# GpSimd begins some of the transfers of an attention, FFN and gated-MLP kernel

## The chip, the cores and the metric

The kernel runs on one core of a Trainium2 chip. The metric is the device time of one execution in microseconds (us); lower is better. Three runs of the kernel before gave a median of 1019.06 us (1018.1 to 1020.91). The profile shows five engines: PE (TensorE) with its weight loads (PEld), DVE (VectorE), ACT (ScalarE), POOL (GpSimd) and SP (SyncE), whose only work here is to begin transfers between the chip's large memory and the on-chip buffers. A transfer is carried out by 16 DMA engines that serve whoever began it.

## The reference

Three blocks follow each other, for 4 batches of 448 tokens and 768 features, in float32:

```python
scores = cap * np.tanh(scale * (q @ k.T) / cap)          # 12 heads of 64, per batch
attn = softmax(scores) @ v                               # x = heads side by side
xn = (x - mean) / sqrt(var + 1e-6) * g_ln
x = x + relu(xn @ w_ch1) @ w_ch2                         # 768 -> 3072 -> 768
h = relu(x @ w_in)                                       # 768 -> 1024, halves u and v
v_s = einsum('ts,bsd->btd', w_spatial, norm(v)) + b_spatial
out = (u * v_s) @ w_out                                  # 512 -> 768
```

`w_ch1` and `w_ch2` are called w1 and w2 below. The weights come to the chip as 64-bit values, so each must be turned into float32 there.

## The kernel before

The batches go in two passes, 0 and 1, then 2 and 3. Four stages make up the first half of the run: attention of batches 0 and 1; then the first FFN matrix for those batches together with the attention of batches 2 and 3 (`h_units`, `attend`); then the second FFN matrix of the first pass (`y_seven`); then the gated MLP (`gmlp`). The second pass has no attention of its own left to do.

Precise float32 products are made of three matmuls on a high and a low part of each operand. The two FFN matrices are multiplied by a scheme with seven block products in place of eight. For that `mixed_h` forms, from four blocks of the middle layer (the output of the first FFN matrix), seven mixed blocks in tiles named hx, and stores all seven to the chip's memory as tensors named h. `y_seven` loads them again (`hs<-h`). There are ten hx tiles, and a group of four blocks takes eight of them; a tile is free again only when its store has landed. There are 12 groups, so 84 stores in the first pass.

The rows of w2 are made ready for `y_seven` beside the first FFN matrix (`ahead`, `value`). Each of the 36 rows is loaded raw (512 KB, into one of two tiles w40 and w41), converted by one instruction of ACT (`wc<-w`) and two of DVE into one of two tiles wc, and stored converted (256 KB, `kept_w<-wc`), from where `y_seven` loads it. Raw rows of w1 (768 KB) go the same way with tiles of their own.

What each engine does, and in which order, is fixed when the program is built. `Program.order` gives every instruction a due time, worked back from PE's order with a cost and a latency for each; `Program.plan` plays the program through and lets each engine take the ready instruction that is due first. In the played model all transfers share one stream of 360 GB/s. An engine then runs its list strictly in order: an instruction that waits holds up everything behind it on that engine. SP has one list of 903 entries, and each of its transfers also waits until the eighth transfer before it has landed. All transfers of the kernel before are begun by SP.

Of the kernel before, what the change touches and what calls it, by code (L numbers as in the profile page):

```python
# [12 lines left out]
I32 = mybir.dt.int32  # L13
# [202 lines left out]
class Program:  # L216
# [93 lines left out]
    def order(self):  # L310
        n = len(self.ops)
        pred = self.edges()
        self.pred, self.succ = pred, [[] for _ in range(n)]
        for i, ds in enumerate(pred):
            for j, at in ds.items():
                self.succ[j].append((i, at))
        self.bufs = []
        for i, (_, writes, reads) in enumerate(self.ops):
            mine = list(dict.fromkeys(a.buf for a in chain(writes, reads) if isinstance(a, View)))
            for b in mine:  # L320
                b.first = i if b.first is None else b.first
                b.last = i
                b.uses += 1
            self.bufs.append(mine)
        self.pools = {b.pool for m in self.bufs for b in m}
        total = 0.0
        due = [float("inf")] * n
        for i in range(n):
            engine, cost = self.ops[i][0][0][:2]
            if engine == "PE":  # L330
                due[i] = total
                total += cost
            elif i in self.soon:
                due[i] = total
        for p in self.pools:
            p.reuse()
        for s in self.stages:
            begins = [b for p in s.pools for b in p.bufs if b.first is not None]
            if s.after and begins:
                first = min(begins, key=lambda b: b.first)  # L340
                for a in s.after:
                    for b in (b for p in a.pools for b in p.bufs if not b.after):
                        assert b.last < first.first
                        b.after.append(first)
        for i in reversed(range(n)):
            engine, cost, latency = self.ops[i][0][0][:3]
            latency += 1.4 if engine == "D" else 0.0
            for j, at in chain(self.succ[i], {(a.first, 0.0) for b in self.bufs[i] for a in b.after}):
                due[i] = min(due[i], due[j] + at * SLACK - (cost + latency + self.DELAY) * SLACK)
            if due[i] == float("inf"):  # L350
                due[i] = total
        return self.plan(due)

    def plan(self, due):

        n = len(self.ops)
# [12 lines left out]
        out = []  # L369
# [59 lines left out]
        while True:  # L429
            for e in ready:  # L430
                if busy[e]:
                    continue
                found = pick(e)
                if found is None:
                    continue
                i, k = found
                taken[i] = True
                out.append((i, k))
                for b in bufs[i]:
                    if b.tile is None:  # L440
                        b.pool.take(b)
                busy[e] = True
                cost, latency = self.ops[i][0][k][1:3]
                if e == "PE":
                    spent += cost
                free[e] = now + cost
                if e == "D":
                    moved = max(moved, now + 1.5) + latency
                    latency = moved + 0.77 - now - cost
                heapq.heappush(events, (now + cost, 0, seq, e))  # L450
                done = now + cost + latency + self.DELAY
                for j, at in succ[i]:
                    heapq.heappush(events, (max(now, done - at), 1, seq, j))
                    seq += 1
                heapq.heappush(events, (done, 2, seq, i))
                seq += 1
            if not events:
                rest = [d for q in ready.values() for d, i, _ in q if not taken[i] and d > reach()]
                if not rest:
                    break  # L460
                relief = min(rest)
                continue
            relief = float("-inf")
            now, kind, _, x = heapq.heappop(events)
            if kind == 0:
                busy[x] = False
            elif kind == 1:
                left[x] -= 1
                if not left[x]:
                    release(x)  # L470
            else:
                for b in bufs[x]:
                    b.left -= 1
                    if not b.left:
                        b.pool.give(b)
                        if b.pool.stage is not None and not b.pool.stage.left:
                            for s in b.pool.stage.then:
                                if not s.open and all(not a.left for a in s.after):
                                    s.open = True
                                    out.append((s, None))  # L480
                                    for p in s.pools:
                                        p.changes += 1
# [16 lines left out]
class Recorder:  # L499
# [3 lines left out]
    def __getattr__(self, method):  # L503
# [5 lines left out]
        def record(*args, **kw):  # L509
# [5 lines left out]
            if self.name == "PE":  # L515
                cost = (n / 2400 + 0.0133) * kw["rhs"].ap[0][1] / 128
                if kw["rhs"].dtype == F32:

                    part = kw["rhs"].ap[0][1] * kw["out"].ap[0][1] / 128 ** 2
                    cost = (4 * n / 2400 + 0.004) * part + (0.004 if part < 1 else 0.0)  # L520
            elif self.name == "D":
                cost, latency = 0.5, 4 * out.size() / 360e3
            elif self.name == "A":
                cost = (0.13 if psum_in else 0.16) + n / 1200
                cost += 0.094 if hasattr(kw.get("scale"), "tensor") else 0.0
            elif self.name == "P":
                cost = 1.3 if "pow" in repr(args) + repr(kw) else 0.7 + n / 500
            elif method == "reciprocal":
                cost = 0.15 + n / 160
            elif method in ("tensor_copy", "tensor_scalar") and not psum_in:  # L530
                cost = 0.14 + n / 1920
            else:
                cost = 0.14 + n / 960
# [12 lines left out]
def attn_ffn_gmlp_kernel(  # L546
# [147 lines left out]
    def value(kind, j, home=None, pool=wr):  # L694
# [7 lines left out]
            SP.dma_start(out=t, in_=kept[kind, j])  # L702
        else:
            raw = raw6[0 if n > DH else 2].get()[:, 0:n]
            SP.dma_start(out=raw.rearrange("p n t -> p (n t)"), in_=source[kind][j].bitcast(I32))
            t = pool.get()[:, 0:n]
            ti = t.bitcast(I32)
            hi, lo = raw[:, :, 1], raw[:, :, 0]
# [20 lines left out]
            if kind == "w2":  # L729
                if j % KD == 0:  # L730
                    kept2.append(dram.tile([128, 2, KD, n // 2], F32, name=f"kept_{kind}_{j}"))
                SP.dma_start(out=kept2[j // KD][:, :, j % KD], in_=t.rearrange("p (a n) -> p a n", a=2))
            else:
                d = kept[kind, j] = dram.tile([128, n], F32, name=f"kept_{kind}_{j}")
                SP.dma_start(out=d, in_=t)
# [320 lines left out]
    def mixed_h(i, h11, h12, h21, h22, t1, t2, t3, t4):  # L1056
# [4 lines left out]
        sub(t4, h21, t2)  # L1061
        for n, t in ((1, h11), (3, h22), (2, h21), (5, t1), (6, t2), (7, t3), (4, t4)):
            hidden[n, i] = dram.tile([128, S], F32, name=f"h{int(last_pass[0])}_{n}_{i}")
            SP.dma_start(out=hidden[n, i], in_=t)

    ysp = []

# [743 lines left out]
```

## Time and profile before

| quantity | value |
|---|---|
| median of three runs | 1019.06 us |
| lowest and highest run | 1018.1 and 1020.91 us |
| span of the profiled execution, first to last instruction | 1016.5 us |
| the profiled execution's own time | not recorded; the median lies 2.56 us above its span |
| PE busy | 1002.0 us (99%) |
| DVE busy | 856.2 us (84%) |
| ACT busy | 565.4 us (56%) |
| POOL busy | 24.3 us (2%), 21 instructions |
| moved by the DMA engines | 248.71 MB, mean 245 GB/s |
| TensorE clock granted | full speed throughout (1.000) |

The span is what the profile divides up; the run's time also holds a little before the first and after the last instruction. Busy PE is a union of modelled intervals, so a small wait can hide in it, but an idle stretch of PE that the profile shows is real time lost.

### The profile page before, as it was taken

The page shows a single profiled execution, that of the slowest core. Times are in us where ns is not written, and L with a number is a line of the kernel's source. Part 1 is how long each engine was busy: PE and PEld are TensorE (multiplying, and loading weights), DVE is VectorE, ACT ScalarE, POOL GpSimd, SP SyncE. Part 2 cuts the span into 40 slices and gives each one's busy share as a digit, 9 for nine tenths or more (in the row PEclk, how much of TensorE's full clock was granted, in tenths as well). Part 3 has the DMA queues.
Part 4 walks back from the last instruction along what each step waited for, and adds up shares of the span by engine and source line. Part 5 has one row for each costly group of instructions (what it writes and reads, how often), then busy time and mean ns, then how long its engine had stood idle before and what let it go on. Part 6 is the DMA issues. An engine that isn't in the chain of part 4 may idle for free.

```text
span 1016.5 us, 14927 instructions
## 1 busy us (share of the span) xinstructions
PE 1002.0 (99%) x5056; PEld 825.9 (81%) x5056; DVE 856.2 (84%) x1476; ACT 565.4 (56%) x897; POOL 24.3 (2%) x21
## 2 busy tenths in 40 slices
PE   7999999999999999999999999999999999999998
PEld 2332787787778889999889899999999999998887
DVE  6989998878888779989889989877788777778986
ACT  7999776776667344545566245544465322214553
POOL 0000110000000000000001110000000000000000
PEclk9999999999999999999999999999999999999999
DMA  8454779999999999999684233565799986602402
GB/s 261 154 139 144 256 279 360 359 337 369 338 370 363 358 341 403 409 329 375 244 259 144 50 133 117 165 203 194 236 336 395 337 267 222 192 21 71 132 17 109
DMA packets 132048, 248.71 MB, mean 245 GB/s; under 512 B 21970, under 2 KB 93828, under 8 KB 131972
## 3 DMA queue, kind: packets, MB, share of 16 engines
q1 hardware_dynamic: 131972, 247.76, 70.9%
q8 instruction: 40, 0.66, 0.3%
q14 instruction: 36, 0.29, 0.1%
HBM read 167.70 MB, written 80.01 MB: 244 GB/s over the span
## 4 chain that ended last, share of the span: by engine, by line
PE 75%; DMA 14%; DVE 5%; ACT 4%; issue 1%; SPq 1%; DVEq 0%; ACTq 0%
PE bank L538 50%; PE two L538 25%; DMA w<-in_w_dram 5%; DMA kept_w<-wc 3%; DMA hs<-inv 2%; ACT es L538 2%; DMA qk<-in_qk_dram 1%; DMA h<-hx 1%; ACT hs L538 1%; DVE x L538 1%; DMA inv<-rc 1%; SPq L538 1%; DVE rs L538 1%; DVE wh L538 1%; DVE small L538 1%
## 5 line engine op out<-in xcount | busy, mean ns | idle before, releaser
L538 PE MATMUL bank<-rs,wh 128*128 128x448 f32 x1704 | 357.1, 363 | 2.5 <-ACT hs L538 2.2
L538 PEld LDWEIGHTS bank<-rs,wh 128*128 128x128 f32 x1704 | 318.2, 187 | 29.9 <-ACT hs L538 4.4
L538 DVE TENSOR_TENSOR rs<-hs,rs 128x448 fp32r<-128x448 f32 x159 | 94.8, 619 | 3.7 <-ACT rs L538 3.1
L538 PE MATMUL two<-rs,wh 128*128 128x448 f32 x414 | 92.7, 362 | 0.0
L538 ACT ACTIVATE rs<-hs 128x448 fp32r<-128x448 f32 x118 | 64.5, 569 | 36.8 <-DMA hs<-h 27.6
L538 PEld LDWEIGHTS two<-rs,wh 128*128 128x128 f32 x414 | 77.6, 188 | 5.2
L538 ACT ACTIVATE es<-es,capt 128x896 f32<-128x896 f32 x72 | 73.5, 1062 | 0.0
L538 DVE TENSOR_TENSOR wh<-wr,wh 128x768 fp32r<-128x768 f32 (+2 forms) x72 | 62.0, 863 | 5.3 <-ACT wh L538 5.1
L538 ACT ACTIVATE es<-two,qsc 128x896 f32<-128x896 f32 x62 | 61.1, 1023 | 7.4 <-PE two L538 7.4
L538 PE MATMUL bank<-es,vt 128*64 128x448 f32 x288 | 62.1, 552 | 0.0
L538 ACT ACTIVATE wh<-wr 128x768 fp32r<-128x768 f32 (+2 forms) x57 | 44.1, 773 | 27.0 <-DVE wr L538 12.6
L538 DVE TENSOR_TENSOR es<-es,es 128x896 f32<-128x896 f32 x48 | 51.9, 1082 | 2.3 <-ACT es L538 1.8
L538 ACT ACTIVATE hs<-bank 128x448 f32<-128x448 f32 x60 | 32.3, 540 | 37.8 <-PE bank L538 31.2
L538 PEld LDWEIGHTS bank<-es,vt 128*64 128x64 f32 x288 | 17.4, 136 | 36.6 <-issue 27.1
L538 PE MATMUL two<-qk 64*128 64x448 f32 x168 | 40.7, 591 | 5.7 <-DMA qk<-in_qk_dram 4.2
L538 ACT ACTIVATE wc<-w 128x512 f32<-128x512 f32 x36 | 24.1, 673 | 29.4 <-DMA kept_w<-wc 14.6
L538 ACT ACTIVATE rs<-x 128x448 fp32r<-128x448 f32 x34 | 19.0, 573 | 37.7 <-DVE x L538 36.5
L538 PEld LDWEIGHTS two<-qk 64*128 64x128 f32 x168 | 14.3, 192 | 29.6 <-ACT es L538 15.0
L538 PE MATMUL two<-wh,rs 128*128 128x512 f32 x144 | 35.8, 395 | 0.1
L538 ACT ACTIVATE wh<-wqm 128x768 fp32r<-128x768 f32 x20 | 16.9, 844 | 32.0 <-PE bank L538 20.0
L538 PE MATMUL bank<-rx,whb 128*128 128x448 f32 x144 | 32.7, 362 | 0.0
L538 PE MATMUL two<-rx,whb 128*128 128x448 f32 x144 | 32.7, 362 | 0.0
(232 smaller groups left out, 1873.2 us busy)
## 6 DMA issues: line engine op xcount, KB each, us to landing
hs<-h SPq DMA_DIRECT2D x168, 224.0 KB, 5.8
h<-hx SPq DMA_DIRECT2D x84, 224.0 KB, 4.9
w<-in_w_dram SPq DMA_DIRECT2D x24, 768.0 KB, 6.8
w<-in_w_dram SPq DMA_DIRECT2D x36, 512.0 KB, 6.2
wqm<-kept_w SPq DMA_DIRECT2D x30, 384.0 KB, 6.2
qk<-in_qk_dram SPq DMA_DIRECT2D x24, 448.0 KB, 5.0
h<-hs SPq DMA_DIRECT2D x48, 224.0 KB, 4.0
kept_w<-wr SPq DMA_DIRECT2D x24, 384.0 KB, 7.5
```

Of the source, the lines that this page charges most:

```text
L538: fn(*(put(a) for a in args), **{k: put(a) for k, a in kw.items()})
```

## The change

POOL begins three kinds of transfers that SP began: the 36 raw loads of w2, the 36 stores of the converted rows, and the 84 stores of h in the first pass. The second pass stores h through SP as before. The planner charges 1.1 us of POOL's time for each (0.5 us of SP's), and its latency terms, so far written for SP alone, hold for every transfer.

```diff
-            latency += 1.4 if engine == "D" else 0.0
+            latency += 1.4 if latency else 0.0
...
-                if e == "D":
+                if latency:
                     moved = max(moved, now + 1.5) + latency
...
-            elif self.name == "D":
-                cost, latency = 0.5, 4 * out.size() / 360e3
+            elif method == "dma_start":
+                cost, latency = 0.5 if self.name == "D" else 1.1, 4 * out.size() / 360e3
...
-            SP.dma_start(out=raw.rearrange("p n t -> p (n t)"), in_=source[kind][j].bitcast(I32))
+            (P if kind == "w2" else SP).dma_start(out=raw.rearrange("p n t -> p (n t)"),
+                                                  in_=source[kind][j].bitcast(I32))
...
-                SP.dma_start(out=kept2[j // KD][:, :, j % KD], in_=t.rearrange("p (a n) -> p a n", a=2))
+                P.dma_start(out=kept2[j // KD][:, :, j % KD], in_=t.rearrange("p (a n) -> p a n", a=2))
...
-            SP.dma_start(out=hidden[n, i], in_=t)
+            (SP if last_pass[0] else P).dma_start(out=hidden[n, i], in_=t)
```

The order of the program moves with it. POOL's list grows from 26 entries to 183, SP's shrinks from 903 to 747, and PE's list stays the same but for a few swaps. The first place is the beginning of POOL's list. Before, after the small fills there, it goes on with the powers for the layer norm (`rstd`), the first of them with an instruction that loads code (ISA) ahead of it; w40_460 and w41_461 below are the two raw tiles of w2, wc0_458 and wc1_459 the converted ones, kept_w2 the stored rows:

```order
L538 MEMSET ones64_124 128x64
L538 MEMSET ones32_125 128x2
L538 MEMSET mhalf_130 128x64
L538 ISA
L538 TENSOR_TENSOR rstd_t0_132<-var_t0_131,mhalf_130 112x4
L538 TENSOR_TENSOR rstd_t1_134<-var_t1_133,mhalf_130 112x4
```

And after, with what each entry waits for (a name that begins with DMASW is a transfer of POOL's own):

```order
L538 MEMSET ones32_125 128x2
L538 DMA w40_460<-in_w2_dram 128x1024
L538 DMA w41_461<-in_w2_dram 128x1024
L538 DMA kept_w2_0_164<-wc0_458 256x1x256 [waits DVE_49]
L538 DMA w40_460<-in_w2_dram 128x1024 [waits DMASW0_49,Activation_49]
L538 DMA w41_461<-in_w2_dram 128x1024 [waits DMASW1_49,DVE_49,Activation_49]
L538 DMA kept_w2_0_164<-wc1_459 256x1x256
L538 DMA h0_1_0_168<-hx0_448 128x448 [waits Activation_49]
L538 DMA kept_w2_0_164<-wc0_458 256x1x256 [waits DVE_49]
```

The first two raw loads of w2 wait for nothing, so POOL begins them right after its fills. Before, they stood in SP's list behind 70 other entries and after waits for the transfers of the heads:

```order
L538 DMA vt0_0_462<-in_v_dram 128x2x192 [waits DMAHW4_49,PE_49]
L538 DMA vt0_0_462<-in_v_dram 64x2x64 [waits DMAHW5_49,PE_49]
L538 DMA w40_460<-in_w2_dram 128x1024 [waits DMAHW6_49]
L538 DMA qk0_446<-in_qk_dram 128x896 [waits DMAHW7_49,PE_49]
L538 DMA w41_461<-in_w2_dram 128x1024 [waits DMAHW0_49]
```

The second place is in the middle of the first FFN matrix. Before, SP's list holds there a converted row's store (kept_w2_24), the raw load that takes the freed tile, and stores of h, with loads of q and k behind them:

```order
L538 DMA kept_w2_18_223<-wc1_459 256x1x256
L538 DMA h0_2_6_237<-hx4_452 128x448
L538 DMA kept_w2_24_244<-wc0_458 256x1x256
L538 DMA w40_460<-in_w2_dram 128x1024
L538 DMA h0_6_6_239<-hx0_448 128x448
L538 DMA qk0_446<-in_qk_dram 128x896
```

After, the same row's store and load stand in POOL's list, in nearly the same company, and the loads of q and k have gone from between them:

```order
L538 DMA kept_w2_18_223<-wc1_459 256x1x256
L538 DMA h0_1_7_247<-hx5_453 128x448
L538 DMA h0_2_6_237<-hx9_457 128x448
L538 DMA kept_w2_24_244<-wc0_458 256x1x256
L538 DMA w40_460<-in_w2_dram 128x1024
```

## Rows read from the trace of the kernel before

**Rows 1.** Busy time by stretch: us, busy us (instructions) per engine, clock, DMA share

```profile
20.00:112.00 92.00, 90.74 (x452) 35.04 (x449) 82.29 (x135) 86.31 (x115) 0.00 (x0) 1.00 0.55 166
112.00:345.00 233.00, 230.73 (x1272) 178.09 (x1271) 195.09 (x316) 160.89 (x234) 8.93 (x2) 1.00 0.97 342
345.00:372.00 27.00, 25.98 (x128) 23.67 (x128) 22.28 (x39) 10.85 (x18) 0.00 (x0) 1.00 1.00 336
372.00:500.00 128.00, 128.00 (x640) 119.98 (x641) 115.13 (x178) 63.98 (x103) 0.00 (x0) 1.00 0.98 365
```

**Rows 2.** Timeline of PE: start us, us, operation, [idle before it <- releaser]

```profile
281.48 1.87 PE L538 MATMUL bank<-rs,wh 128*128 128x448 f32 x8 [1.00 <-ACT hs L538]
...
371.01 0.67 PE L538 MATMUL two<-rs,whm 128*128 128x448 f32 x2 [0.70 <-ACT whm L538]
```

**Rows 3.** Timeline of ACT and DVE, 264 to 284 us, rows of w2

```profile
270.58 0.69 DVE L538 SCALAR_TENSOR_TENSOR wc<-w,wc 128x512 int32<-128x512 int32 x1
...
280.33 0.67 ACT L538 ACTIVATE wc<-w 128x512 f32<-128x512 f32 x1 [1.80 <-DMA w<-in_w_dram]
```

**Rows 4.** Timeline of SP's queue, 269 to 281 us: start, issue us

```profile
272.67 1.25 SPq L538 DMA_DIRECT2D h<-hx  x1
274.02 0.97 SPq L538 DMA_DIRECT2D kept_w<-wc  x1
275.09 0.56 SPq L538 DMA_DIRECT2D w<-in_w_dram  x1
```

**Rows 5.** Waits of ACT, 112 to 372 us: total us, times, longest

```profile
ACT wc L538 <- DMA kept_w<-wc: 13.2, 7, 3.4
...
ACT wc L538 <- DMA w<-in_w_dram: 10.4, 7, 2.3
```

**Rows 6.** Waits of SP's queue, 112 to 345 us

```profile
SPq L538 <- DMA w<-in_w_dram: 33.7, 35, 2.1
```

**Rows 7.** Timeline of the first 12 us: PE and ACT

```profile
9.56 0.97 PE L538 MATMUL bank<-qk 64*64 64x448 f32 x4 [0.33 <-DMA qk<-in_qk_dram]
...
11.53 1.01 ACT L538 ACTIVATE es<-two,qsc 128x896 f32<-128x896 f32 x1 [1.02 <-PE two L538]
```

**Rows 8.** Busy time by stretch at the start (last two columns: DMA share, GB/s)

```profile
4.00:6.00 2.00, 1.76 (x6) 0.94 (x8) 0.32 (x2) 0.00 (x0) 0.00 (x0) 1.00 0.76 283
...
8.00:10.00 2.00, 1.67 (x8) 0.20 (x4) 1.61 (x3) 2.00 (x3) 0.00 (x0) 1.00 1.03 383
```

**Rows 9.** Timeline of POOL: the first two powers of the layer norm

```profile
122.50 7.92 POOL L538 TENSOR_TENSOR rstd_t<-var_t,mhalf 112x4 f32<-112x4 f32 x1 [121.11 <-ACT es L538]
152.75 1.02 POOL L538 TENSOR_TENSOR rstd_t<-var_t,mhalf 112x4 f32<-112x4 f32 x1 [22.33 <-DMA var_t<-var]
```

**Rows 10.** Timeline of ACT, 112 to 160 us: conversions of w2 around the first power

```profile
131.71 1.21 ACT L538 ACTIVATE wc<-w 128x512 f32<-128x512 f32 x2
...
148.79 0.66 ACT L538 ACTIVATE wc<-w 128x512 f32<-128x512 f32 x1
```

**Rows 11.** DVE by shape, 120 to 345 us: busy us, mean ns | idle before

```profile
L538 DVE TENSOR_SCALAR wc<-wc 128x512 int32<-128x512 int32 x31 | 13.1, 423 | 17.3 <-ACT wc L538 17.2
L538 DVE TENSOR_SCALAR wr<-wr 128x768 int32<-128x768 int32 x20 | 10.9, 552 | 1.1 <-ACT wr L538 1.0
```

**Rows 12.** Transfers by kind: count, KB each, median us from issue to landing

```profile
h<-hx SPq DMA_DIRECT2D x84, 224.0 KB, 4.9
...
w<-in_w_dram SPq DMA_DIRECT2D x36, 512.0 KB, 6.2
...
kept_w<-wc SPq DMA_DIRECT2D x36, 256.0 KB, 4.9
```

**Rows 13.** Instructions on tile wc: ns min/median/max, first and last start us

```profile
L538 ACT ACTIVATE wc<-w x36: 639/670/708, 96.0 to 344.7; 128x512 f32<-128x512 f32 x36
```

**Rows 14.** Timeline of SP's queue, 356 to 365 us

```profile
357.64 1.61 SPq L538 DMA_DIRECT2D h<-hx  x3
...
363.92 1.32 SPq L538 DMA_DIRECT2D wqm<-kept_w  x3
```

## The prediction

> **What bounds the kernel now.** I read the page's first part, then the busy times by stretch, then the timelines of PE, ACT and SP where PE stands idle. PE is busy for 1002.0 us of a span of 1016.5, at full clock, so 14.5 us are all that any reordering can win. The change acts in two stretches, the start (below) and 112 to 372 us, the stretch of the first FFN matrix up to the start of the second. There PE is idle for 233 - 230.73 = 2.27 us and for 27 - 25.98 = 1.02 us, 3.29 us in all, and after it, from 372 to 500 us, for nothing [rows 1]. The 16 DMA engines are taken for 0.97 to 1.00 of the same time: two resources are nearly full, and the change takes no byte from the second.
>
> How PE loses its time there is seen at 281 us. DVE was done with a row of w2 at 270.58 + 0.69 = 271.27 us [rows 3]. SP began that row's store at 274.02 and the next raw load into the freed tile at 275.09, 3.8 us later, because it was working through stores ahead of them [rows 4]. ACT, in its fixed order, then waited 1.80 us for that load before it could go on to empty PE's banks [rows 3], and PE lost 1.00 us [rows 2]. ACT waited 13.2 + 10.4 = 23.6 us for stores and loads of w2 in this way [rows 5], and SP itself 33.7 us for loads that had to land before it might begin another transfer [rows 6].
>
> **The change part by part.** The sum is made against the span of 1016.5 us; the median of the runs lies 2.56 us above it, and I carry that over.
>
> *The two first raw loads.* POOL begins them at the start, since nothing holds them there; SP had them behind 70 entries. They are 2 x 512 KB = 1.05 MB and are wanted only when ACT converts the first row, at 96.0 us [rows 13], so their earliness wins nothing. They share the DMA engines with the first loads of q and k. From 8 to 10 us these engines are full at 383 GB/s, from 4 to 6 us a share of 0.24 is free [rows 8]. PE waits for the second load of q and k at 9.56 us, and ACT after it, until 11.53 us [rows 7]. All bytes put ahead of that load cost 1.05 MB / 0.383 = 2.7 us, less 0.24 x 2 = 0.5 us of free share: 2.2 us. It is not won back, for from 20 to 112 us ACT is busy for 86.31 of 92 us [rows 1] and the heads follow one another through it. The low end is 0, if POOL's first transfer only gets going once the second load of q and k is in; the high end is 2.7. I take 2.2, since POOL's list has only fills ahead of the loads.
>
> *154 transfers through POOL in place of SP* (156 with the first two). No transfer is on POOL in this trace. From below, SP's issue of a raw load took 0.56 us [rows 4]; from above, POOL's longest instruction, its first power, took 7.92 us, and the next one 1.02 [rows 9]. I take 1.02, the nearest thing that POOL does in its ordinary state. Then 156 x 1.02 = 159 us lie on POOL between 96.0 us [rows 13] and the last stores of h at 359 us [rows 14], 60% of 263 us, and the queue keeps up. At 156 x 1.69 it is full.
>
> *What SP's queue gives back.* In the case at 281 us the raw load on POOL has the row's store ahead of it, and at most two stores of h besides. It begins between 271.27 + 1.02 = 272.3 and 271.27 + 3 x 1.02 = 274.3 us, 0.8 to 2.8 us earlier than on SP, against a wait of ACT of 1.80. So a wait of this kind shrinks or goes. All 3.29 us is the ceiling; nothing is the other end, as the DMA engines are full and a load begun earlier then takes its time in their queues. I take half, 1.6 us. A loss in this step is the first rival.
>
> *The first power.* It now stands in a queue with transfers behind it and holds them for up to 7.92 us at about 122 us [rows 9]. The row of w2 loaded then is converted at 148.79 us, 16 us after the two at 131.71 [rows 10], so 6.2 us for landing [rows 12] still fit: nothing. If that cover went, ACT would wait some of the 7.92.
>
> *The tail.* The tiles for the second FFN matrix (wqm) take the memory of hx and wc, and their first loads began at 363.92 us, when SP's last stores of h, begun by 359.25 [rows 14], had landed in about 4.9 us [rows 12]. PE's 0.70 us at 371.01 hang on one of them [rows 2]. On POOL these stores no longer wait behind SP's loads of h, but cost more each; the two ends are 1.0 us won, already in the 3.29, and about 1 us lost per transfer that POOL is behind. I take nothing.
>
> Sum: 1016.5 + 2.2 - 1.6 = 1017.1, and with 2.56 around it **1019.7 us**.
>
> **A rule against the change.** DVE's in-place shifts of rows take 423 ns for 512 columns and 552 ns for 768, 51 of them, 24.0 us in all [rows 11]. The Trainium skill ("SBUF — State Buffer", section "SBUF: two separate sides") says that the descriptors of a transfer begun by GpSimd are written by GpSimd's own cores, that these share a port pair with VectorE, and that a VectorE operation in a 2-port mode and GpSimd shut each other out for a whole instruction. It gives about 620 ns for such a transfer alone and 3100 ns beside a VectorE copy; at an estimate by that page of 3.1 us each, 156 would take 484 us of POOL, far more than 263. No row here shows a transfer on POOL beside such an operation. If POOL only waits out the 24.0 us, it holds 159 + 24 = 183 us of work and still keeps up, and the sum stands.
>
> **The rivals.**
>
> *POOL falls behind (slower).* If a transfer takes POOL over 1.69 us, its queue is full from about 96 us on; hx and wc tiles come free late, ACT and DVE stand before them, and PE with them. At 1.75 us the stores are through 156 x 1.75 = 273 us after 96.0, 10 us late: 1016.5 + 2.2 + 10 + 2.56 = 1031 us. For it: ten hx tiles with eight in use by each group, and the fixed lists. Against it: 60% at the nearest row, and ACT and DVE idle for 72 and 38 of the 233 us [rows 1].
>
> *DVE is held up (slower).* If each of the 51 shifts waits for a whole POOL instruction, DVE gains 51 x 1.02 = 52 us of work in the stretch, against 37.9 us idle there [rows 1]: 14 us beyond it, 1016.5 + 2.2 + 14 + 2.56 = 1035 us. It decides from 37.9 / 51 = 0.74 us per shift. Against it: POOL would have to be in a transfer nearly always.
>
> *The start costs and nothing comes back (just slower).* 2.7 us at the start, none of the 3.29, and one transfer of delay in the tail: 1016.5 + 2.7 + 1.0 + 2.56 = 1022.8 us. For it: the DMA engines are full, so an earlier start of a load is no earlier landing.
>
> *The start is free and the gaps close (faster).* POOL's first loads come after the second load of q and k, and all 3.29 us return: 1016.5 - 3.3 + 2.56 = 1015.8 us. Against it: both must hold at once.
>
> **How the numbers follow.** A measurement of this kernel can tell 0.3%, 3.06 us, from no change: 1016.0 to 1022.1. I give the forecast 0.52, with a range of its own from 1016.5 to 1022; POOL behind 0.18; DVE held up 0.08; the start alone 0.11; both gains 0.11. So faster 0.11, same 0.52, slower 0.37. The time is the forecast's, 1019.7. The range goes from 1016 to 1031: it leaves out half of the gains' case below and the longer times of the first two rivals above, under 2 in 10.
>
> **What would show it.** In the profile after: the second load of q and k would be waited for at about 11.8 in place of 9.56 us, and every later step up to 112 us would come some 2.2 us late. POOL would show 156 transfers of about 1 us, busy for some six tenths from 96 to 359 us. ACT's waits for w2 would be well under 23.6 us and PE's idle time from 112 to 372 us under 2 us. I am wrong if the first matmuls come no later, if POOL's slices from 100 to 360 us read 9, if DVE's shifts spread out to a microsecond each, or if PE shows more than 5 us of idle time in that stretch.

## The result and the profile after

The changed kernel takes **1027.0 us** (median of 6 runs, 1026.07 to 1029.24) against 1019.02 (6 runs beside it, 1018.1 to 1021.48): a ratio of **1.0083 [1.0066, 1.0100]**, some 8 us slower. That lies in the predicted range, but the forecast itself, no change at 1019.7 us, was wrong. The profiled execution has a span of 1027.5 us and took 1029.24 itself, the longest of the six, so 1.74 us lie around the span.

First the busy times by stretch, with the columns of [rows 1].

```profile
0.00:20.00 20.00, 11.50 (x30) 3.21 (x32) 6.68 (x12) 8.22 (x10) 2.03 (x10) 0.83 0.70 220
20.00:112.00 92.00, 88.41 (x441) 29.77 (x442) 81.90 (x132) 87.91 (x115) 2.48 (x4) 1.00 0.49 149
112.00:345.00 233.00, 230.12 (x1257) 179.31 (x1257) 194.84 (x317) 160.82 (x235) 84.55 (x135) 0.99 0.92 339
345.00:372.00 27.00, 27.00 (x140) 23.27 (x137) 21.94 (x40) 11.70 (x20) 10.55 (x19) 1.00 1.03 380
```

New are the clock of 0.83 in the first 20 us and the loss from 20 to 112 us (3.59 us idle, 1.26 before). From 112 to 372 us PE is idle for 2.88 us, nearly the 3.29 of before, but the clock of 0.99 there hides one more stretch of half speed (below). POOL is busy for 95 of these 260 us, so its queue is far from full.

Next the start on PE's timeline (columns as in [rows 2]; the first line answers to the first of [rows 7]), and the granted clock of its second half.

```profile
13.54 1.76 PE L538 MATMUL bank<-qk 64*64 64x448 f32 x4 [4.41 <-DMA qk<-in_qk_dram]
...
17.02 2.88 PE L538 MATMUL bank<-es,vt 128*64 128x448 f32 x8
```

```profile
10.00:15.00 5.00, 1.46 (x4) 0.29 (x4) 3.83 (x6) 0.36 (x1) 0.00 (x0) 0.76 0.89 328
15.00:20.00 5.00, 5.00 (x16) 1.44 (x16) 2.47 (x4) 2.86 (x4) 0.00 (x0) 0.56 0.40 93
```

PE waits 4.41 us for the second load of q and k and starts at 13.54 in place of 9.56 us. After that idle time its four matmuls take 1.76 us in place of 0.97, and the granted clock reads 0.76 and then 0.56: part of the time at the lower level, 1.2 GHz. Both add up to a delay of 6.5 us.

POOL's timeline (start, us, operation) shows what stands at the start and what the second power of the layer norm does to the queue; the line of ACT below it is the wait that follows, the line of PE what comes of it.

```profile
1.37 1.31 POOL L538 DMA_DIRECT2D w<-in_w_dram  x2
...
129.31 1.37 POOL L538 TENSOR_TENSOR rstd_t<-var_t,mhalf 112x4 f32<-112x4 f32 x1 [6.15 <-DMA var_t<-var]
...
161.36 4.80 POOL L538 TENSOR_TENSOR rstd_t<-var_t,mhalf 112x4 f32<-112x4 f32 x1
166.13 0.67 POOL L538 DMA_DIRECT2D kept_w<-wc  x1
166.78 0.59 POOL L538 DMA_DIRECT2D w<-in_w_dram  x1
```

```profile
174.55 0.66 ACT L538 ACTIVATE wc<-w 128x512 f32<-128x512 f32 x1 [5.51 <-DMA w<-in_w_dram]
```

```profile
175.69 12.67 PE L538 MATMUL bank<-rs,wh 128*128 128x448 f32 x54 [1.96 <-ACT hs L538]
```

Behind this wait the granted clock falls a second time. The next row has the columns of [rows 1]; the same 54 matmuls took 11.08 us at full clock in the kernel before, so 1.6 us are lost here in time that counts as busy.

```profile
176.00:180.00 4.00, 4.00 (x14) 3.60 (x13) 4.00 (x8) 3.28 (x5) 1.92 (x4) 0.57 0.86 322
```

The waits of ACT from 112 to 372 us (us, times, longest) and of SP's queue from 112 to 345 us, to be held against [rows 5, 6]:

```profile
ACT wc L538 <- DMA w<-in_w_dram: 16.5, 8, 5.5
...
ACT wc L538 <- DMA kept_w<-wc: 5.9, 5, 1.9
```

```profile
SPq L538 <- DMA w<-in_w_dram: 4.2, 4, 1.7
```

ACT waits as long in all as before (22.4 us against 23.6), but the longest single wait has grown from 3.4 to 5.5 us. SP's waits for the transfer eight places ahead have all but gone (33.7 to 4.2 us), in part because the raw loads of w2 are no longer in its list.

Last the groups of POOL and of DVE's shifts (busy us, mean ns, idle before), and the landing times that answer to [rows 12].

```profile
L538 POOL DMA_DIRECT2D h<-hx x84 | 48.7, 610 | 39.1 <-DVE hx L538 29.1 <-ACT hx L538 3.6 <-issue 2.3
...
L538 POOL DMA_DIRECT2D kept_w<-wc x36 | 25.4, 706 | 156.1 <-DVE wc L538 155.4 <-issue 0.4 <-DMA h<-hx 0.3
...
L538 POOL DMA_DIRECT2D w<-in_w_dram x36 | 22.5, 628 | 62.7 <-DVE wc L538 23.2 <-ACT hs L538 9.8 <-ACT es L538 9.3
...
L538 DVE TENSOR_SCALAR wc<-wc 128x512 int32<-128x512 int32 x36 | 15.3, 426 | 12.9 <-ACT wc L538 12.7
...
L538 DVE TENSOR_SCALAR wr<-wr 128x768 int32<-128x768 int32 x24 | 13.0, 543 | 0.7 <-ACT wr L538 0.7
```

```profile
h<-hx POOLq DMA_DIRECT2D x84, 224.0 KB, 7.4
w<-in_w_dram POOLq DMA_DIRECT2D x36, 512.0 KB, 7.7
...
kept_w<-wc POOLq DMA_DIRECT2D x36, 256.0 KB, 6.8
```

A transfer holds POOL for 0.61 to 0.71 us, less than the 1.02 taken, and DVE's shifts are as fast as in [rows 11]. What got worse is the landing: 7.4, 7.7 and 6.8 us against 4.9, 6.2 and 4.9.

### The profile page after: what moved, and what is told of

It is laid out like the page before. It is cut to its first block, busy times and chain, and to the rows that moved or that the text cites. A ratio compares the mean times of both kernels' runs of the same rounds, so it can differ in the third digit from the quotient of the medians.

```text
span 1027.5 us, 15010 instructions
## 1 busy us (share of the span) xinstructions
PE 1006.4 (98%) x5056; PEld 827.9 (81%) x5056; DVE 856.4 (83%) x1478; ACT 562.8 (55%) x894; POOL 115.5 (11%) x178
## 4 chain that ended last, share of the span: by engine, by line
PE 85%; DVE 6%; DMA 4%; ACT 2%; issue 2%; POOL 1%; SPq 0%; DVEq 0%; ACTq 0%; POOLq 0%
PE bank L538 59%; PE two L538 25%; DVE x L538 1%; DMA w<-in_w_dram 1%; DMA qk<-in_qk_dram 1%; DVE es L538 1%; ACT es L538 1%; DVE rs L538 1%; ACT hs L538 1%; DMA hs<-inv 1%; DVE hs L538 1%; DMA hs<-std 1%; DVE small L538 0%; DVE hx L538 0%; POOL qkg L538 0%
## 5 line engine op out<-in xcount | busy, mean ns | idle before, releaser
L538 POOL TENSOR_TENSOR small<-small,mhalf 128x4 f32<-128x4 f32 (+1 forms) x4 | 4.6, 1158 | 553.0 <-DVE small L538 553.0
L538 POOL DMA_DIRECT2D h<-hx x84 | 48.7, 610 | 39.1 <-DVE hx L538 29.1
L538 POOL DMA_DIRECT2D kept_w<-wc x36 | 25.4, 706 | 156.1 <-DVE wc L538 155.4
```

Source lines behind the costliest of these rows:

```text
L538: fn(*(put(a) for a in args), **{k: put(a) for k, a in kw.items()})
```

## The experiments

Both kernels have the same 5056 matmul records in almost the same order. The delay of PE at a place is worked out as the start of the n-th of them minus its start in the profile of before (single profiles, and executions of one kernel lie up to 11 us apart, so a row tells where that one execution was late):

```
at, in before (us)            16    57   100   131   166   201   239   329   391   596   end
after                        6.5   6.5   8.0   9.5  12.3  13.1  13.1  10.8   8.8  10.6  10.7
two first loads back on SP   0.8   0.8   0.9   2.9   5.5   7.2   7.2   5.9   3.9   6.5   6.4
old plan, two loads on POOL  5.2   5.2   8.4   8.1   8.1   8.1   8.1   7.9   6.8   7.3   7.5
moved plan, all on SP        0.0   0.4   0.9   0.6   0.6   0.8   0.8  -1.4  -3.0   0.3   0.6
own plan, h alone on POOL    1.0   2.1   3.3   3.4   3.4   4.2   4.8   4.4   2.3   4.2   5.0
old plan, h alone on POOL    2.4   2.5   1.8   1.5   1.5   4.9   8.4   7.7   6.4   6.2   6.6
```

Of the 10.7 us of the changed kernel 8.4 have come up by 112 us (by the same reckoning), before POOL's first store of h at 113.81 us; 0.5 are added up to 372 us and the rest behind that.

All times, with the ratio to the kernel before in the same series (its median was 1019.62 us beside e1, e2, e5 and e6, 1019.30 beside e3, e4, e7 and e8, 1019.27 beside e9 to e11 and 1017.89 beside e12). "Own" is an order that the planner made with the new costs for that kernel:

| kernel | on POOL | plan | us (range, runs) | ratio |
|---|---|---|---|---|
| changed kernel | loads, rows, h | own | 1027.0 (1026.1 to 1029.2, 6) | 1.0083 [1.0066, 1.0100] |
| e1 | as that, but the two first loads on SP | as the changed one | 1024.9 (1024.1 to 1025.2, 5) | 1.0049 [1.0037, 1.0061] |
| e2 | the two first loads alone | before | 1025.1 (1021.6 to 1026.1, 6) | 1.0047 [1.0032, 1.0061] |
| e5 | stores of rows and h | own | 1026.1 (1024.3 to 1028.4, 4) | 1.0069 [1.0051, 1.0088] |
| e6 | nothing | as the changed one | 1022.8 (1018.9 to 1025.3, 10) | 1.0028 [1.0013, 1.0043] |
| e3 | loads from the third, rows | own | 1020.1 (1017.6 to 1024.5, 12) | 1.0007 [0.9991, 1.0023] |
| e4 | h | own | 1024.2 (1022.5 to 1027.0, 12) | 1.0045 [1.0029, 1.0062] |
| e7 | e2, PE kept busy | before | 1021.7 (1020.0 to 1025.8, 12) | 1.0023 [1.0007, 1.0038] |
| e8 | e1, products for powers | as e1 | 1025.4 (1023.5 to 1027.4, 6) | 1.0053 [1.0032, 1.0074] |
| e9 | one row's store, late | before | 1019.2 (1016.8 to 1020.8, 10) | 0.9997 [0.9985, 1.0009] |
| e10 | loads from the third, rows, h | before | 1026.9 (1022.7 to 1029.0, 6) | 1.0068 [1.0046, 1.0090] |
| e11 | changed kernel, PE kept busy | own | 1027.3 (1024.0 to 1033.3, 6) | 1.0092 [1.0062, 1.0122] |
| e12 | h | before | 1027.7 (1021.6 to 1032.3, 6) | 1.0099 [1.0067, 1.0131] |

### e1 and e2: the two first loads, taken back and alone

e1 is the changed kernel with

```diff
-            (P if kind == "w2" else SP).dma_start(out=raw.rearrange("p n t -> p (n t)"),
+            (P if kind == "w2" and j >= 2 else SP).dma_start(out=raw.rearrange("p n t -> p (n t)"),
```

and e2 the kernel before, its transfers planned as in the changed one (the order on PE, DVE and ACT comes out as before), with

```diff
-            SP.dma_start(out=raw.rearrange("p n t -> p (n t)"), in_=source[kind][j].bitcast(I32))
+            (P if kind == "w2" and j < 2 else SP).dma_start(out=raw.rearrange("p n t -> p (n t)"),
```

> The changed kernel with one thing undone: the first two raw loads of w2 are begun by SP again, at their old place in its list; every other list is the same. Start theory (two unguarded loads delay the second load of q and k, PE idles 4.4 us and its clock falls to half): the shift of 6.5 us seen at 45 to 53 us goes, so 1027.0 - 6.5 = 1020.5 us (1019 to 1022), PE's wait at the start back to about 0.3 us. Stretch theory (what costs is POOL's queue from 100 to 372 us: raw loads behind the power of the layer norm): the time stays above 1024 us.

> The kernel before with one thing added: only the first two raw loads of w2 are begun by POOL, at the head of its list; every other list is the same and all other transfers stay with SP. Start theory: 1019.0 + 6.5 = 1025.5 us (1024 to 1027), PE waiting some 4.4 us at about 13.5 us and a granted clock near 0.8 in the first 20 us. Stretch theory: 1019 to 1021 us, since nothing of POOL's later queue is there.

Alone, the two loads cost 5.5 us, near the 6.5 of the theory of the start. PE's timeline of e2 has the same wait as the changed kernel:

```profile
13.19 1.76 PE L538 MATMUL bank<-qk 64*64 64x448 f32 x4 [3.87 <-DMA qk<-in_qk_dram]
```

Taken back (e1), they give only 2.1 us, and 5.2 are still lost against the kernel before in its series. So the start is one cause and not the only one, and the two do not add up to 10.7 but to 8.0.

### e5 and e6: raw loads back on SP; everything back on SP under the moved plan

e5 is the changed kernel with every raw load begun by `SP`, for which the planner made a new order of ACT and DVE. e6 is the changed kernel with its order untouched, where a transfer planned for POOL is begun by SP:

```diff
-        fn = getattr(self.engine, method)
+        fn = getattr(self.program.nc.sync if self.name == "P" and method == "dma_start" else self.engine, method)
```

> The changed kernel with all 36 raw loads of w2 begun by SP; the 36 stores of converted rows and the 84 stores of h stay with POOL. If raw loads held up behind the power on POOL cost something of their own (1.96 us of PE idle at 175.69 us and a half clock behind it), this is 1 to 3 us faster than the kernel that only gives the first two loads back to SP. If the stores on POOL were what costs, it is as slow as that or slower. Start theory alone: 1019 to 1021 us.

> The changed kernel's plan with all its transfers begun by SP when it runs: the order on every engine is that of the changed plan, POOL's transfers stand in SP's list at the time the plan gives them. If the moved order of ACT and DVE were the cause, 1024 us or more. Start theory: the two raw loads are again behind other entries of SP, so 1018 to 1022 us.

e5 is no faster than e1: the loss is still there with no raw load on POOL, though under another order, so this doesn't settle it alone. e6 scatters widely, 1018.9 to 1025.3 us. Its profile, an execution of 1018.98 us, leaves PE idle for 0.17 us from 112 to 372 us:

```profile
112.00:372.00 260.00, 259.83 (x1419) 205.74 (x1418) 220.32 (x357) 175.12 (x254) 16.45 (x2) 1.00 0.98 345
```

The moved order can close all the gaps of before and still costs some 3 us in the median. A part is seen in this profile, behind the stretch: PE is 3.0 us early at 391 us and 0.3 late at 596, and 1.8 us of that are a wait for DVE at 587 us (first line) where the kernel before waits 0.24 (second line).

```profile
587.44 3.89 PE L539 MATMUL bank<-rs,wh 128*128 128x448 f32 x18 [1.79 <-DVE qkg L539]
```

```profile
586.23 0.68 PE L538 MATMUL bank<-rs,wh 128*128 128x448 f32 x2 [0.24 <-DVE rs L538]
```

The same wait stands in every profile of the changed kernel's order, 0.92 to 1.79 us long (the changed kernel, e1, e6, e8, e11), and in e4 and e5, and in none under the old order. So the planner's new order has a cost of its own, some 200 us behind the last transfer that was moved. What the executions of e6 above 1022 us lose besides stays open.

### e3 and e4: rows alone, h alone

e3 is e1 with `SP.dma_start(out=hidden[n, i], in_=t)`; e4 is the kernel before with the planner's edits and `(SP if last_pass[0] else P)` there alone. Each has the plan that comes of it.

> POOL begins only the transfers of w2 rows (raw loads from the third on, and the 36 stores of converted rows); the two first raw loads and all stores of h are with SP. Theory 'round of a row': what costs in the stretch is the longer round of a w2 tile through POOL (store and load land some 2 us later each), so this still has most of the 5.2 us that the run with only the two loads back on SP lost: 1023 to 1025 us, ACT's waits for w over 15 us from 96 to 215 us. Rival 'stores of h': hx tiles come free late because 84 stores of h land 2.5 us later and stand in POOL's queue; then without them the time is near the kernel before: 1019 to 1021 us.

> POOL begins only the 84 stores of h in the first pass; all transfers of w2 rows are with SP. Theory 'round of a row': with rows on SP their round is 11.1 us again, and hx has ten tiles with eight in use, so little is lost: 1019 to 1021.5 us. Rival 'stores of h': this carries the loss of the stretch: 1023 to 1025 us, with ACT or DVE waiting on hx and h.

The theory of the longer round of a row falls and its rival holds: 70 transfers of rows through POOL cost nothing that can be told (1.0007 [0.9991, 1.0023]), the 84 stores of h 4.9 us. The expected sign, waits for hx tiles, isn't there, though. In e4 it is ACT's waits for rows, all transfers of which are with SP, that grow, to 39.1 us against 23.6; and its delay doesn't come up between 112 and 372 us: it is 3.4 us at the first and 2.4 at the second, so e4 alone doesn't clear its own order of the loss. e12 below takes that up.

```profile
ACT wc L538 <- DMA kept_w<-wc: 26.2, 14, 3.4
ACT wc L538 <- DMA w<-in_w_dram: 12.9, 8, 3.7
```

### e7: the clock at the start

On top of e2's edit:

```diff
                     T.matmul(out=sc[place(j)], lhsT=t[r, S + TAIL:2 * S], rhs=t[r, 0:S], start=True, stop=True)
+                if i == j == 0:
+                    prog.open[0][0][3] += prog.open[0][0][3][-2:] * 6
```

> As the run of the kernel before with the two first raw loads on POOL (1025.1 us); in addition TensorE repeats the four matmuls ahead of its wait for the second q and k load three times (12 more matmuls of the same data into the same place, some 3 us), so that it isn't idle for 3.87 us there. Theory 'wait and clock': of the 5.2 us that PE was late at 16 us in that run 3.6 are the wait and 1.5 come from half-speed matmuls after the idle time (four took 1.76 us in place of 0.97); with PE kept busy the clock is full again by 13 us, so PE is 3.6 us late at 20 us and the time is about 1023.6. Rival 'the wait alone': the slow matmuls would have been hidden behind ACT, the time stays at 1025.1.

PE's timeline at the start of e7, where the 28 records are the four of before and 24 more (six repeats of the four, not the three of the expectation):

```profile
7.18 5.48 PE L538 MATMUL bank<-qk 64*64 64x448 f32 x28
13.52 0.97 PE L538 MATMUL bank<-qk 64*64 64x448 f32 x4 [0.86 <-DMA qk<-in_qk_dram]
```

The load comes no earlier, but the four matmuls behind it run at full speed, and PE is 4.0 us late at 20 us in place of 5.2. The median falls by 3.4 us to 1021.7, further than the 1.5 expected, and the loss against the kernel before from 5.5 to 2.4; the intervals of the two ratios just overlap, so how much of it hung on PE's having stood idle isn't settled. The profiled execution took 1024.5 us, well above the median, and there the gain on e2's profile (1026.07) is 1.6 us, of which 1.2 are those of the start.

### e8: does a power hold POOL's queue?

```diff
+            swap = self.name == "P" and ALU.pow in args and out.ap[0][1] == 112
...
-                fn(*(put(a) for a in args), **{k: put(a) for k, a in kw.items()})
+                fn(*(ALU.mult if swap and a is args[-1] else put(a) for a in args), **{k: put(a) for k, a in kw.items()})
```

> As the run with the two first raw loads back on SP (1024.9 us), every list the same; only the two small power instructions of POOL for the layer norm (112x4) are products of the same operands instead, so the layer norm's values are left out. Theory 'a power holds POOL's queue': there POOL was in the second power from 155.24 to 160.02 us while the row's store had been ready since 157.33; the store and the raw load behind it begin 2.7 us earlier, ACT's wait of 5.95 us at 168.57 shrinks to about 3.3, PE's idle 2.55 us at 169.72 goes nearly to nothing: about 1022.4 us. Rival 'landing': a row's round (store landed, next load landed) is 14.7 us through POOL (6.8 + 7.9) against 11.1 through SP, and ACT is late by that, power or not: ACT's waits for w stay near 18 us from 96 to 215 us and the time stays at 1024.9, within 0.7.

The time stays, but the experiment didn't take the hold away: a plain product at the same place, right behind five transfers, kept POOL for nearly as long as the power did.

```profile
155.25 3.96 POOL L540 TENSOR_TENSOR rstd_t<-var_t,mhalf 112x4 f32<-112x4 f32 x1
```

So it isn't the power, and what the hold costs stays untested. Nor is it settled that the transfers ahead make it: in e6, where POOL begins no transfer, the same power took 7.85 us at 153.41, and in e10, right behind a transfer, 1.15 us at 156.29.

### e9: does a queue of POOL's slow the start by being there?

In the runs without early loads on POOL PE still waited 1.07 to 1.96 us at the start (e8 to e3). e9 is the kernel before with `PQ = Recorder(prog, "D", nc.gpsimd)`, which plans as SP and begins on POOL, for one late store:

```diff
-                SP.dma_start(out=kept2[j // KD][:, :, j % KD], in_=t.rearrange("p (a n) -> p a n", a=2))
+                (PQ if j == 35 else SP).dma_start(out=kept2[j // KD][:, :, j % KD], in_=t.rearrange("p (a n) -> p a n", a=2))
```

> The kernel before with one transfer alone on POOL, the store of the last converted row of w2 (past 300 us); every list of an engine is that of before otherwise. Open since the runs without early POOL loads: there, too, with SP's first entries the same, PE waited 1.28 to 1.96 us for the second load of q and k (0.33 before), and the DMA engines moved 178 to 234 GB/s from 4 to 6 us (283 before); with the moved plan but all transfers on SP they did not. Theory 'a queue of POOL's own in the program slows the first transfers, used or not': the wait is 1.2 us or more and the early matmuls come 0.8 to 1 us late, time 1020 to 1020.5. Rival 'it takes many transfers on POOL' (their place, their number): the wait is 0.33 us, as before, and the time 1019.3.

```profile
10.10 0.97 PE L538 MATMUL bank<-qk 64*64 64x448 f32 x4 [1.69 <-DMA qk<-in_qk_dram]
```

```profile
4.00:6.00 2.00, 1.78 (x6) 0.97 (x8) 0.32 (x2) 0.00 (x0) 0.00 (x0) 1.00 0.86 172
```

The wait and the slow bytes (172 GB/s against the 283 of [rows 8]) are there, 300 us ahead of POOL's only transfer; the time isn't touched. PE is 0.5 us late at 20 us, less than the 0.8 to 1 expected, and this is made up later. In e3 and e12 the same wait, 1.96 and 2.40 us long, was followed by a lower granted clock (0.91 over the first 20 us), and PE was 2.3 and 2.4 us late, so a small part of the loss can begin here.

### e10 and e12: POOL's queue under the old plan

e10 begins the loads from the third on, the rows and h through `PQ`; e12 only h:

```diff
-            SP.dma_start(out=hidden[n, i], in_=t)
+            (SP if last_pass[0] else PQ).dma_start(out=hidden[n, i], in_=t)
```

> The plan of the kernel before; its transfers of w2 rows (raw loads from the third on, stores of rows) and the first pass's stores of h are begun by POOL, in the order that SP's list had. With the runs 'moved plan, all on SP' (1022.8) and 'moved plan, POOL, two first loads on SP' (1024.9) and the kernel before (1019.3) this is the fourth corner. Theory 'queue': POOL's part is what costs in the stretch, the plan little: 1023.5 to 1025 us. Rival 'plan': the moved order costs some 3 us and POOL's queue some 1 to 2: 1020 to 1021.5 us.

> The plan of the kernel before, all transfers of w2 rows on SP as before; only the first pass's 84 stores of h are begun by POOL, in the order of SP's old list. The run with h alone on POOL and a plan of its own took 1024.2 us, the one with the rows alone 1020.1. Theory 'stores of h': taken out of SP's queue they leave SP free to begin other loads earlier, these share the DMA engines with the raw loads that ACT waits for, and a few single waits of ACT get long: 1022.5 to 1025 us under the old plan too, with the longest wait of ACT for w2 between 112 and 372 us over 3.4 us and PE idle there for more than 2.27 us. Rival 'plan': the 4.9 us of that run came from its own order; under the old one the stores cost little: 1019 to 1020.5 us.

Both rivals of a moved order fall: with nothing moved, 154 transfers on POOL cost 7.6 us and the 84 stores of h alone 9.8, both more than the theories said (that the moved order costs something too is seen in e6). The orders that the planner made for POOL's cost are better than the old one at that (e4 against e12: 4.9 us lost against 9.8; e1 against e10: 5.2 against 7.6, within the scatter). e12 shows the mechanism plainest, since every transfer of a row is where it was. Its waits from 112 to 372 us, ACT and SP:

```profile
ACT wc L538 <- DMA kept_w<-wc: 13.5, 8, 2.9
...
ACT wc L538 <- DMA w<-in_w_dram: 12.1, 4, 7.3
```

```profile
SPq L538 <- DMA w<-in_w_dram: 17.7, 14, 2.1
```

One wait of 7.3 us stands out. This is the place in ACT's, SP's and POOL's timelines of e12, and then the same place in ACT's and SP's of the kernel before:

```profile
202.53 0.66 ACT L538 ACTIVATE wc<-w 128x512 f32<-128x512 f32 x1 [7.33 <-DMA w<-in_w_dram]
```

```profile
189.09 1.59 SPq L538 DMA_DIRECT2D w<-in_w_dram  x2
190.78 0.56 SPq L538 DMA_DIRECT2D qk<-in_qk_dram  x1
191.39 0.93 SPq L538 DMA_DIRECT2D kept_w<-wc  x1
192.42 1.24 SPq L538 DMA_DIRECT2D qk<-in_qk_dram  x1
```

```profile
189.98 3.28 POOL L538 DMA_DIRECT2D h<-hx  x6 [18.89 <-DVE hx L538]
193.92 1.07 POOL L538 DMA_DIRECT2D h<-hx  x2 [0.66 <-DVE hx L538]
```

```profile
194.87 0.66 ACT L538 ACTIVATE wc<-w 128x512 f32<-128x512 f32 x1 [1.75 <-DMA w<-in_w_dram]
```

```profile
186.28 0.56 SPq L538 DMA_DIRECT2D w<-in_w_dram  x1
187.86 0.33 SPq L538 DMA_DIRECT2D h<-hx  x1
188.44 0.33 SPq L538 DMA_DIRECT2D w<-in_w_dram  x1
188.95 4.95 SPq L538 DMA_DIRECT2D h<-hx  x5
194.83 0.33 SPq L538 DMA_DIRECT2D qk<-in_qk_dram  x1
```

In both, ACT waits for the first of two raw rows. Before, it was begun at 186.28 us and there by 194.87, at most 8.6 us; in e12 it was begun at 189.09 and came at about 202.5, 13.4 us. In the 6 us after it began, SP had begun one raw row and three stores of h before: 512 + 3 x 224 = 1184 KB. In e12 the two queues began one raw row, eight stores of h, two loads of q and k and a row's store: 512 + 1792 + 896 + 256 = 3456 KB. The 2272 KB more are close to 7 us of work (an estimate) at the 340 GB/s that the DMA engines moved on the mean from 186 to 206 us of e12. Landing times of single transfers in e12's trace, each that of a transfer's last part, show that they don't queue up behind it:

```
begun (us)            189.09 w (SP)   189.98 h (POOL)   190.51 h (POOL)   191.66 h (POOL)   191.39 kept_w (SP)
landed                by 202.5        196.79            197.71            199.92            205.50
```

Stores of h that POOL began later land up to 5.7 us before the row that SP began first. PE pays for it right behind:

```profile
203.67 0.47 PE L538 MATMUL bank<-rs 64*128 64x448 f32 x1 [1.08 <-ACT hx L538]
...
205.70 0.74 PE L538 MATMUL bank<-rs 64*128 64x448 f32 x1 [1.56 <-ACT hx L538]
...
208.65 16.08 PE L538 MATMUL bank<-rs,wh 128*128 128x448 f32 x72 [1.47 <-DVE hs L538]
```

The three waits are 4.1 us, but PE's delay grows here from 1.5 to 8.4 us, by 6.9. Most of the rest is the clock: the trace has it granted at half from 204.9 to 211.7 us (first row, columns of [rows 1]), and the last group, at full clock in the kernel before (second row), takes 1.4 us more than there.

```profile
205.00:211.00 6.00, 3.83 (x11) 2.98 (x12) 6.00 (x10) 4.92 (x8) 0.00 (x0) 0.50 0.87 297
```

```profile
201.65 14.68 PE L538 MATMUL bank<-rs,wh 128*128 128x448 f32 x72
```

This one place is more than the 6.6 us that e12's profile is late at its end. Idle time of PE alone, 5.39 us from 112 to 372 us against 3.29 before, would have shown a third of it. The clock over a whole execution points the same way in e10: its two executions at 1.000 took 1022.7 and 1022.9 us, the four at 0.997 and 0.998 took 1026.5 to 1029.0.

### e11: the changed kernel with PE kept busy

The edit of e7, on the changed kernel.

> The changed kernel; TensorE repeats the four matmuls ahead of its wait for the second q and k load three times, as in the earlier run of that kind. There that took 3.4 us off 1025.1. Theory 'clock': the same half-speed matmuls stand in the changed kernel (granted clock 0.76 and 0.56 from 10 to 20 us), so 2 to 3.4 us go: 1023.6 to 1025 us, PE 4 us late at 20 us in place of 6.5. Rival 'swallowed later': the waits of the later stretch take up what the start gives back: 1026 to 1027 us.

The median, 1027.3 us, is the rival's, but six executions from 1024.0 to 1033.3 us can't tell a gain of 3 us from none. In the profiled one, of 1025.8 us, PE was 3.5 us late at 20 us in place of 6.5 and 7.2 at the end in place of 10.7, so there the gain of the start was kept. Between the two theories the run stays undecided.

## Where the prediction held and where it failed

**What was right, and what was luck.** The time lies in the range, by luck: the range reached to 1031 us for POOL falling behind and for DVE held up, and neither happened. The forecast's own 1016.5 to 1022 missed. The rival nearest to what happened, that the start costs and nothing comes back, was given 0.11 and said 1022.8 us, 4.2 short.

**What bounds the kernel.** That PE and the DMA engines are both nearly full held (engines' share 0.92 to 0.98 from 112 to 345 us). That ACT's waits for rows of w2 make PE's gaps was seen again at the two places followed here, the changed kernel at 175.69 us and e12 at 203.67.

**The two first loads** were the right mechanism at less than half its size, and the term that missed by most in the changed kernel's profile: 2.2 us taken, 6.5 lost at 20 us and 8.4 at 112, 5.5 in the time of e2. PE's start is 4.0 us later (13.54 against 9.56), with the engines moving 139 GB/s from 4 to 6 us and not the 283 of [rows 8] with a quarter free; e9, where one late transfer on POOL goes with 172, suggests that not all of this is the bytes of the two loads. The rest up to 20 us is PE's clock after the idle time, which the sum left out.

**What SP's queue gives back is the step that failed in its sign.** It took 1.6 us, half of 3.29, as won because a raw load would be begun 0.8 to 2.8 us earlier. It looked at one load's begin. SP's one list, with at most eight transfers under way, had also held back what came behind: [rows 6] was read as a loss of SP's, and at the place followed in e12 it kept the row in front. With h in a second queue ACT's longest wait for a row grew (5.5 us in the changed kernel, 7.3 in e12) and nothing was won: PE's delay changes between 112 and 372 us by +0.5 us in the changed kernel, +2.3 in e1 and e10, +3.2 in e5, +4.6 in e12 and +4.8 in e8, all with h on POOL, and by -1.0 in e3, -1.6 in e2 and -3.9 in e6, without it. Two profiles don't fit, e4 with -1.0 and e11 with -2.8, and PE's idle time there doesn't tell the kernels apart (3.29 us before, 2.41 in e4, 1.61 in e3). That the stores of h cost rests on the times of e3, e4, e10 and e12; that the cause is the crowding is shown at one place, in e12, and inferred for the others. The signs alone don't prove it: SP's waits for the eighth transfer shrink in e3 too (18.8 us), and ACT's longest wait for a row there is 3.8 us, with no loss.

**What the sum had no term for.** Matmuls at half speed behind a wait, at the start and in the stretch, and the new order's own wait behind the stretch (at 597.73 us in the changed kernel, 0.92 us long); 1.8 us of the changed kernel's delay come up behind 372 us.

**What would show it.** Of the signs named beforehand POOL's share (37% from 112 to 372 us, not six tenths), ACT's waits (22.4 us, not well under 23.6) and PE's idle time (2.88, not under 2) came out otherwise, but none of those that were to prove the forecast wrong appeared: the first matmuls did come later (by 4.0 us, where 2.2 were forecast), POOL's slices stayed far from 9, DVE's shifts kept their length, and PE's idle time stayed under 5 us. The watch was on idle time in one stretch; the loss lay in the first 112 us, in matmuls at half speed and in gaps that took the place of others.

**The price per transfer** (1.02 taken, 0.61 to 0.71 measured) and with it the rival "POOL falls behind" went the safe way: the kernel is nearly as slow as that rival said, for another reason.

**The powers.** The first, counted at up to 7.92 us of hold, took 1.37; the second, in [rows 9] 1.02 us long, took 4.80 and held a raw load for which ACT then waited 5.51. Nothing was counted, and no run separates what the hold cost.

**The tail** held: from 345 to 372 us PE is never idle now.

**DVE held up**, the rule of the Trainium skill ("SBUF — State Buffer", section "SBUF: two separate sides"): DVE's shifts take 426 and 543 ns, as in [rows 11], and POOL's transfers 610 to 706 on the mean. That is near the 620 ns that the Trainium skill gives for such a transfer alone and far from its 3100. No shutting out of either shows here.

**Around the span** 2.56 us were carried over; the changed kernel's profiled execution has 1.74, and executions of the kernel before beside the experiments have 1.8 to 2.0. So the profile of before was of an execution some 0.7 us shorter than the median.

**What stays open.** The start alone costs 5.5 us, the rest alone 5.2 (e1) to 7.6 (e10), both 8.0, and why they don't add up is open; e11 doesn't settle it. Of the 3 us that e6 loses with no transfer on POOL, the wait at 587 us explains a part. Whether any second queue crowds the rows, or POOL's kind, no run tests: the profile lists POOL's transfers as q0 software_dynamic, 64 packets for each store of h (5376 for 84 in e12), and SP's as q1 hardware_dynamic, where the same stores made 144 each, so the two differ in more than their order. No run moved h to another engine's queue. Nor is it known when the granted clock falls: it fell behind 1.96 us of idle PE at 175.69 us in the changed kernel and stayed full behind 2.55 us at 169.72 in e1. No run beat the kernel before: e3 and e9 equal it.

## What to carry to other kernels

A transfer moved to a second queue, here POOL's, is not only begun by another engine: it leaves the order and the limit of the first. Where the DMA engines are full, ask which urgent load that limit was protecting, and leave bulk stores that nobody waits for soon in the queue where they wait their turn. Look at the longest single wait, not at the sum, against the slack that PE's buffers give, and at the granted clock behind PE's waits, since matmuls at half speed count as busy. A load that nothing guards starts at once (1.37 us here) and competes with the loads that the first matmul needs.

## What the runs showed of the hardware that was not expected

- Transfers begun by POOL took 610 to 706 ns of it in the changed kernel, and landed after 7.4, 7.7 and 6.8 us where SP's landed after 4.9, 6.2 and 4.9.
- Transfers of POOL's queue overtook one begun earlier by SP, by up to 5.7 us (e12).
- An instruction of 112x4 on POOL right behind its transfers took 3.96 us as a product (e8) and 4.80 as a power (the changed kernel at 161.36 us), but 1.15 right behind a transfer in e10 and 7.85 without any transfer in e6; what makes it long isn't known.
- A program with a single, late transfer on POOL moved 172 GB/s from 4 to 6 us where the one without moved 283 (e9).
- After 3.87 to 4.41 us without work PE's matmuls ran at half speed, the granted clock reading 0.56 to 0.76, for up to 6.8 us (12.6 to 19.4 us in the changed kernel); 24 repeated matmul records in that time kept them at full speed (e7). In e12, 4.1 us of waits between 202 and 209 us went with 6.8 us at half the clock.
